# A Mamba-2 block and an ELU layer on one core: seven products in place of eight for half of the first two blocks' second layer, and 512-column products in their first layer

## The chip, the cores and the metric

The kernel runs on one core of one Trainium2 chip. A core has TensorE (PE: matrix products, with its weight loads listed as PEld), VectorE (DVE), ScalarE (ACT), GpSimd (POOL) and SyncE (SP), which here only issues DMA transfers. The engines run side by side, each working through its own instructions in order. The metric is the device time of one execution in microseconds (us); the time before is the median of three runs.

## The reference

```python
x = scan(x, a, B, C)          # (4, 8, 768, 32): Mamba-2 scan, state 16
x = x.transpose(0, 2, 1, 3).reshape(3072, 256)
h = x @ w_in                  # (3072, 256) @ (256, 2048)
g = np.where(h > 0.0, h, np.exp(np.minimum(h, 0.0)) - 1.0)
out = g @ w_out               # (3072, 2048) @ (2048, 256)
```

All is float32 (the inputs reach the chip as 64-bit words, and the kernel makes float32 of the weights). The change is in the last three lines.

## The kernel before

The 3072 tokens are cut into 12 blocks of 256 (NP = 12, BLK = 256). A block n goes through the scan, whose result is yT, then the first layer, the ELU and the second layer. The order of all work on every engine is written out by hand: the order in which the Python code issues instructions is the order in which each engine runs them. A tile of a pool with `bufs` buffers waits for the tile that had the buffer before.

**First layer.** The 2048 columns of w_in are 16 groups of 128. `l1(n, i)` (line 631) makes groups 2i and 2i+1 for block n into one PSUM tile ps_h of 128x512, two products (k = 0, 1) for each group, 256 tokens wide. With `parts=2` it does so in halves of 128 tokens. It appends (n, i, ps_h) to the list `lag`; `elu` (line 654) takes the oldest entry, does two ACT passes and one DVE pass (lines 652, 659, 661) and leaves `g_of[n, i]` (128x512) in SBUF. Each float32 product in the source is two PE instructions and two weight loads in the profile.

**Second layer, direct.** `l2(n, j)` (line 753) takes groups 2j and 2j+1 of block n: four products 256 columns wide into the single PSUM tile ps_o of pool p_o. After j = 7 ACT copies it to `ob` and SP stores it.

**Both layers by seven products (Strassen-Winograd).** Blocks 2 and 3, 4 and 5 and so on are taken as pairs: two blocks by two halves of the contraction by two halves of the columns, a 2x2 problem with seven products in place of eight. It needs sums of the stationary and of the moving operands: `sum_weights` (line 677) makes four additions (s3, a21, s2, s4) for each of the eight index pairs i of w_out (`a_out`, `s_out`) or of w_in (`a_in`, `s_in`); `sum_t1` and `sum_t2` (lines 786, 790) make the differences of the g quarters; `sum_y` (line 701) those of yT. `quarters` (line 778) names the four quarters of the g tiles of a pair. `second(n)` (line 798) is a generator for the pair n, n+1: for each half of the contraction it goes through the seven products r = 0 to 6, four index pairs i each, and yields after each i. At the end of an r it adds the result to `c_sum` in parts: additions that read PSUM on DVE, the others on POOL (line 812), two copies on ACT (lines 841, 853), and the differences of g that later products need on POOL (line 776). `front`, `mid` and `back` are the first layer by seven products, from n = 4 on.

**Order around the change.** First a loop of twelve steps issues the rest of the first layer of blocks 0 and 1, with the scan of block 2 and the conversion of weight pieces 5 to 10. A weight piece (`w_take`, `w_give`) is one of 16 (8 of w_in, 8 of w_out): two ACT passes, three DVE passes and one POOL addition. Then comes a loop over n = 2, 3 and i = 0 to 7: each step issues `l2(n - 2, i)` and `l1(n, i)` on PE, drains `lag` and does some scan work of later blocks: in n = 2 the pieces 11 to 15, decays on ACT and POOL (`decay`, lines 493, 498), head masks and transposes on DVE (`turn_part`); at the third step of n = 3 `scores`, `sums`, eight weighings and the states of blocks 4 and 5; at the seventh their `across` and `inside`, and after these `sum_y(4)`. `more_sums(i - 1)` in n = 3 makes the weight sums of both layers (w_out on DVE, w_in on POOL) and sum_t1(2, i - 1). After the loop POOL does sum_t2(2, 0), and from n = 4 on each stage interleaves the first layer of the pair n, n+1 with `second(n - 2)`; `store` (line 880) writes c_sum.

PSUM has seven buffers in pool p_a (ps_h, scores, sums, across, and every second product of `second`) and one in p_o (the direct ps_o, and the other products of `second`).

Of the kernel before, what the change touches and what calls it, by code (L numbers as in the profile page):

```python
# [28 lines left out]
def kernel(  # L29
# [598 lines left out]

    g_of = {}

    def l1(n, i, parts=1):

        ps = psum([P, 2, BLK], "ps_h")
        for j in range(2):
            m = 2 * i + j
            for part in range(parts):
                toks = slice(part * BLK // parts, (part + 1) * BLK // parts)
                for k in range(KC):
                    nc.tensor.matmul(  # L639
                        out=ps[:, j, toks], lhsT=w_in[:, k, m * P:(m + 1) * P],  # L640
                        rhs=yT[n // 2][:, k, n % 2].rearrange("p u i -> p (u i)")[:, toks],
                        start=(k == 0), stop=(k == KC - 1))
        lag.append((n, i, ps))

    lag = []
# [31 lines left out]
    def sum_weights(eng, a, s, i):  # L677
        for step in weight_steps(eng, a, s, i):
            step()
# [67 lines left out]
    def row_of(n):  # L747
        b, g = place(n)
        return b * S + g * BLK

    o_of = {}

    def l2(n, j, half=None):


        if j == 0 and half != 1:
            o_of[n] = p_o.tile([P, 2, DM], F32, tag="o", name="ps_o")
        for m in (2 * j, 2 * j + 1) if half is None else (2 * j + half,):
            for ts in range(2):
                nc.tensor.matmul(  # L760
                    out=o_of[n][:, ts], lhsT=g_of[n, j][:, m % 2, ts * P:(ts + 1) * P],
                    rhs=w_out[:, m], start=(m == 0 and ts == 0), stop=(m == MC - 1),
                    skip_group_check=True)
        if j == MC // 2 - 1 and half != 0:
            ob = ffn.tile([P, 2, DM], F32, tag="ob", name="ob", bufs=1)
            nc.scalar.copy(out=ob, in_=o_of.pop(n))
            r0 = row_of(n)
            nc.sync.dma_start(
                out=out[r0:r0 + BLK, :].rearrange("(t p) e -> p t e", p=P), in_=ob)

    t2_of = {}

    def sub(out, in0, in1):
        nc.gpsimd.tensor_tensor(out=out, in0=in0, in1=in1, op=ALU.subtract)  # L776

    def quarters(n, i):


        A, B = g_of[n, i], g_of[n + 1, i]
        if n < 4:
            return A[:, 0], A[:, 1], B[:, 0], B[:, 1]
        return A[:, 0], B[:, 0], B[:, 1], A[:, 1]

    def sum_t1(n, i, eng=nc.gpsimd):
        b11, b21, b12, b22 = quarters(n, i)
        eng.tensor_tensor(out=b12, in0=b12, in1=b11, op=ALU.subtract)  # L788

    def sum_t2(n, half):  # L790
        for i in range(4 * half, 4 * half + 4):
            t2_of[n, i] = ffn.tile([P, BLK], F32, tag="t2", name="t2", bufs=4)
            b11, b21, b12, b22 = quarters(n, i)
            sub(t2_of[n, i], b22, b12)

    c_of = {}

    def second(n, last=False):


        c = c_of[n] = ffn.tile([P, 2, 2, 2, P], F32, tag="c", name="c_sum", bufs=1)
        c11, c12, c21, c22 = (c[:, at, :, e] for e in range(2) for at in range(2))
        a11, a12, s1, a22 = a_out
        s2, s3, s4 = s_out
        for half in range(2):
            tmp = ffn.tile([P, 3, 2, P], F32, tag="tmp", name="p_sum", bufs=1)
            p1, p5, u = (tmp[:, r] for r in range(3))
            chunk = range(4 * half, 4 * half + 4)
# [5 lines left out]
            for r, a in enumerate((a11, a12, s1, s2, s3, a22, s4)):  # L814
# [25 lines left out]
                if r == 0:  # L840
                    nc.scalar.copy(out=p1, in_=ps)
                    for i in chunk:
                        b11 = quarters(n, i)[0]
                        sub(b11, t2_of[n, i], b11)
                    if half:
                        add(c11, c11, p1)
                elif r == 1:
                    add(c11, ps, c11 if half else p1)
                    for i in chunk:
                        b21 = quarters(n, i)[1]  # L850
                        sub(b21, b21, t2_of[n, i])
                elif r == 2:
                    nc.scalar.copy(out=p5, in_=ps)
                elif r == 3:
                    add(u, ps, p1)
                    add(p5, p5, u)
                    if half:
                        add(c22, c22, p5)
                        add(c12, c12, p5)
                elif r == 4:  # L860
                    add(c22, ps, c22 if half else p5)
                    add(u, ps, u)
                    if half:
                        add(c21, c21, u)
                    if last and half:
                        r0 = row_of(n + 1)
                        nc.sync.dma_start(
                            out=out[r0:r0 + BLK, P:2 * P].rearrange("(t p) c -> p t c", p=P),
                            in_=c22)
                    if not half:  # L870
                        sum_t2(n, 1)
                    elif n + 2 < NP:
                        sum_t2(n + 2, 0)
                elif r == 5:
                    add(c21, ps, c21 if half else u)
                else:
                    add(c12, ps, c12 if half else p5)
# [126 lines left out]
    write_flat(2)  # L1004

    todo = 5
    for s, (n, i) in enumerate((
            (1, 0), (1, 1), (1, 2), (0, 4), (1, 3), (0, 5), (1, 4), (0, 6), (1, 5), (0, 7),
            (1, 6), (1, 7))):
        l1(n, i, parts=2 if s < 2 else 1)  # L1010
        if s < 8:
            decay_of(2, s)
        if s == 7:
# [108 lines left out]
            at = k // 2 * 2 + late  # L1122
            turn_part(*[(m, 0), (m, 1), (m, 2), (m + 1, 0), (m + 1, 1), (m + 1, 2), (m, 3), (m + 1, 3)][at])

    def more_sums(i):
        sum_weights(nc.vector, a_out, s_out, i)
        sum_weights(nc.gpsimd, a_in, s_in, i)
        sum_t1(2, i, nc.vector)


    for n in (2, 3):
        for i in range(8):
            if n == 3 and i > 0:
                more_sums(i - 1)
            l2(n - 2, i)
            piece = todo < len(pieces) and (n, i) != (2, 1)
            if n == 2 and i == 0:
                elu()
            if piece:
                w_take(todo, nc.scalar if i > 1 else nc.vector)  # L1140
            end_of_two(n, 2 * i)
            l1(n, i)
            if n == 2 and i == 0:
# [9 lines left out]
            if n == 2:  # L1153
# [7 lines left out]
                        weigh(3, q)  # L1161
                if i == 2:
                    states(3)
                if i == 6:
                    inside(across(3), 3)
            else:
                if i == 0:
                    s_in[:], s_out[:] = weight_sums(), weight_sums()
            scan_ahead(n, i)
            end_of_two(n, 2 * i + 1)  # L1170
    sum_t2(2, 0)
    left = weight_steps(nc.vector, a_out, s_out, 7)

    for n in range(4, NP, 2):
        m = n + 2 if n + 2 < NP else None
# [13 lines left out]
        for k in range(16):  # L1189
# [29 lines left out]
                begin_elu()  # L1219
            else:  # L1220
                mid(n, i)
                if i == 0 and n > 4:
                    store(n - 4, 0)
                    store(n - 4, 1)
                begin_elu()
# [3 lines left out]
                next_elu()  # L1229
                begin_elu()  # L1230
                turn_step(n, k, True)
                if n == 4 and i < 4:
                    next(left)()
                    if i == 0:
                        sum_weights(nc.gpsimd, a_in, s_in, 7)
                        sum_t1(2, 7)
                if not m or i < 4:
                    l2s(1)
            if m:
# [42 lines left out]
```

## Time and profile before

| | |
|---|---|
| median of three runs | 356.01 us (355.25 to 356.28) |
| profiled execution, whole | 355.13 us |
| its span | 353.2 us |
| granted TensorE clock | 1.00 |
| second-layer products, direct, 128x256 (L760) | 128 instructions, 30.7 us |
| second-layer products, seven, 128x128 (L834) | 1104 instructions, 142.5 us |
| first-layer products, direct, 128x256 (L639) | 240 instructions, 56.5 us |
| first-layer products, direct, 128x128 (L639) | 32 instructions, 4.0 us |
| differences of g on POOL (L776, L788) | 153 operations, 109.7 us |
| the same on DVE (L788) | 7 operations, 3.4 us |

The profile is of one execution by the hardware profiler; its span leaves out 1.9 us of what the whole time counts. A row's busy time is what its instructions cover; matmuls overlap, so a row's mean is longer than its pace. In time, the loop of twelve steps ends at 52 us on PE, the steps of n = 2 run from 52 to 82.7, those of n = 3 from 82.7 to 114.8, and n = 4 begins there.

### The profile page before, as it was taken

How to read it: one execution, taken by the hardware profiler on the slowest of the kernel's cores; microseconds unless marked ns; L12 is line 12 of the kernel's file. 1: busy time of each engine (PE TensorE's matmuls, PEld its weight loads, DVE VectorE, ACT ScalarE, POOL GpSimd, SP SyncE). 2: the span in 40 equal slices, each digit the busy share in tenths (PEclk: the TensorE clock that was granted, in tenths of full speed). 3: DMA queues.
4: the chain of work that ended last, by engine and by line, in shares of the span. 5: the costliest groups of instructions: out<-in, count | busy, mean ns of one | idle time of the engine just before them, and what ended most of it. 6: DMA issues, size and time to landing. Idle time of an engine off the chain costs nothing.

```text
span 353.2 us, 9965 instructions
## 1 busy us (share of the span) xinstructions
PE 347.2 (98%) x3960; PEld 313.1 (89%) x3960; DVE 239.5 (68%) x497; ACT 204.8 (58%) x497; POOL 230.2 (65%) x365
## 2 busy tenths in 40 slices
PE   8899999999999999999999999999999999999996
PEld 5579788888888999999999999999999999999996
DVE  4998879863999768684677684677684565656212
ACT  4878989787435577535677535586635444535100
POOL 5454554553676997887377788468687545465883
PEclk9999999999999999999999999999999999999999
DMA  8878789572440500136500145600000100000101
GB/s 147 209 207 178 264 184 256 90 143 52 72 141 2 121 0 3 18 80 146 122 0 2 14 90 128 134 3 0 2 2 2 62 3 0 2 0 30 32 2 59
DMA packets 74542, 26.49 MB, mean 75 GB/s; under 512 B 59840, under 2 KB 69376, under 8 KB 74496
## 3 DMA queue, kind: packets, MB, share of 16 engines
q1 hardware_dynamic: 72176, 25.60, 31.5%
q8 instruction: 31, 0.51, 0.6%
q10 hardware_dynamic: 2320, 0.26, 0.5%
q14 instruction: 15, 0.12, 0.1%
HBM read 22.51 MB, written 3.34 MB: 73 GB/s over the span
## 4 chain that ended last, share of the span: by engine, by line
PE 87%; DVE 0%; issue 0%
PE ps_o L834 35%; PE ps_h L711 28%; PE ps_h L639 10%; PE ps_o L760 8%; PE ps_y L607 2%; PE ps_g L513 2%; PE ps_y L588 1%; PE ps_st L543 1%; PE ps_o L820 1%; DVE c_sum L823 0%; PE ps_tc L401 0%; PE ps_tb L401 0%
## 5 line engine op out<-in xcount | busy, mean ns | idle before, releaser
L652 ACT ACTIVATE e<-ps_h 128x512 f32<-128x512 f32 x96 | 57.2, 596 | 91.1 <-DVE ps_h L736 49.1
L834 PEld LDWEIGHTS ps_o<-w_out,g 128*128 128x128 f32 x640 | 79.9, 192 | 2.9
L834 PE MATMUL ps_o<-w_out,g 128*128 128x128 f32 x640 | 81.0, 275 | 0.0
L661 DVE SCALAR_TENSOR_TENSOR g<-e,ps_h 128x512 f32<-128x512 f32 x96 | 65.1, 680 | 14.2 <-ACT e L659 13.8
L659 ACT ACTIVATE e<-e 128x512 f32<-128x512 f32 x96 | 61.1, 636 | 2.0
L639 PE MATMUL ps_h<-yT,w_in 128*128 128x256 f32 (+1 forms) x272 | 60.4, 370 | 1.4 <-ACT w_in L192 0.9
L788 POOL TENSOR_TENSOR g<-g 128x256 f32<-128x256 f32 x33 | 24.0, 728 | 54.8 <-DVE g L661 54.7
L639 PEld LDWEIGHTS ps_h<-yT,w_in 128*128 128x128 f32 x272 | 48.5, 190 | 8.6 <-POOL w_in L230 2.1
L493 ACT ACTIVATE L<-L,ncum 128x64 f32<-128x64 f32 x160 | 41.3, 340 | 0.9 <-DMA L<-flat 0.8
L834 PE MATMUL ps_o<-w_sum,g 128*128 128x128 f32 x304 | 39.9, 275 | 0.0
L834 PEld LDWEIGHTS ps_o<-w_sum,g 128*128 128x128 f32 x304 | 38.5, 192 | 1.1
L744 DVE TENSOR_TENSOR ps_h<-ps_h,u_sum 128x512 f32<-128x512 f32 x32 | 22.4, 699 | 23.9 <-PE ps_h L711 23.7
L711 PE MATMUL ps_h<-yT,w_in 128*128 128x256 f32 x128 | 38.5, 383 | 0.0
L711 PE MATMUL ps_h<-y_sum,w_in 128*128 128x256 f32 x128 | 38.1, 380 | 0.0
L711 PE MATMUL ps_h<-y_sum,w_sum 128*128 128x256 f32 x128 | 38.1, 379 | 0.0
L498 POOL TENSOR_SCALAR_AFFINE_SELECT L<-L 64x512 f32<-64x512 f32 x40 | 28.0, 701 | 11.5 <-ACT L L493 10.2
L728 DVE TENSOR_TENSOR u_sum<-ps_h,u_sum 128x512 f32<-128x512 f32 x32 | 22.1, 690 | 14.7 <-ACT u_sum L721 11.0
L736 DVE TENSOR_TENSOR ps_h<-ps_h,u_sum 128x256 f32<-128x256 f32 x32 | 13.8, 433 | 25.7 <-PE ps_h L711 25.4
L760 PE MATMUL ps_o<-w_out,g 128*128 128x256 f32 x128 | 30.7, 382 | 0.0
L776 POOL TENSOR_TENSOR t<-g 128x256 f32<-128x256 f32 x40 | 28.9, 755 | 0.2
L776 POOL TENSOR_TENSOR g<-g,t 128x256 f32<-128x256 f32 x40 | 28.8, 753 | 0.2
L776 POOL TENSOR_TENSOR g<-t,g 128x256 f32<-128x256 f32 x40 | 28.0, 732 | 1.1 <-PE ps_o L834 1.1
(116 smaller groups left out, 535.4 us busy)
## 6 DMA issues: line engine op xcount, KB each, us to landing
L<-flat SPq DMA_DIRECT2D x20, 256.0 KB
w<-in_moe_w_out_dram SPq DMA_DIRECT2D x8, 512.0 KB
w<-in_moe_w_in_dram SPq DMA_DIRECT2D x7, 512.0 KB
xr<-in_x_dram SPq DMA_DIRECT2D x24, 128.0 KB
out_dram<-c_sum SPq DMA_DIRECT2D x9, 256.0 KB
bc<-in_B_dram SPq DMA_DIRECT2D x24, 64.0 KB
bc<-in_C_dram SPq DMA_DIRECT2D x22, 64.0 KB
ec<-flat_exp SPq DMA_DIRECT2D x10, 128.0 KB
```

The costliest lines, as they stand in the source:

```text
L493: nc.scalar.activation(L[:, h, u], L[:, h, u], ACT.Exp, bias=ncum[:, u, row:row + 1])
L498: nc.gpsimd.affine_select(out=part, in_=part, pattern=[[0, 4], [0, 2], [1, Q]], compare_op=ALU.is_ge, fill=0.0, base=0, channel_multiplier=-1)
L639: nc.tensor.matmul(out=ps[:, j, toks], lhsT=w_in[:, k, m * P:(m + 1) * P], rhs=yT[n // 2][:, k, n % 2].rearrange("p u i -> p (u i)")[:, toks],
L652: nc.scalar.activation(begun[0], lag[0][2], ACT.Relu, scale=-1.0)
L659: nc.scalar.activation(e, e, ACT.Exp, scale=-1.0)
L661: nc.vector.scalar_tensor_tensor(out=g_of[n, i], in0=e, scalar=1.0, in1=ps, op0=ALU.subtract, op1=ALU.max)
L711: nc.tensor.matmul(out=out, lhsT=lhsT, rhs=rhs, start=first, stop=True, skip_group_check=True)
L744: nc.vector.tensor_tensor(out=c2, in0=c2, in1=u[:, 0:2], op=ALU.add)
L760: nc.tensor.matmul(out=o_of[n][:, ts], lhsT=g_of[n, j][:, m % 2, ts * P:(ts + 1) * P], rhs=w_out[:, m], start=(m == 0 and ts == 0), stop=( ...
L776: nc.gpsimd.tensor_tensor(out=out, in0=in0, in1=in1, op=ALU.subtract)
L788: eng.tensor_tensor(out=b12, in0=b12, in1=b11, op=ALU.subtract)
L834: nc.tensor.matmul(out=ps[:, ts], lhsT=b[:, ts * P:(ts + 1) * P], rhs=a[:, i], start=(i == chunk[0] and ts == 0), stop=(i == chunk[-1]), s ...
```

## The change

1. Loop of twelve: the first four steps are `l1(1, 0)` to `l1(1, 3)`, without halves. The other eight are `l1_two(i, j)` for i = 4 to 7: one group, 2i + j, for blocks 0 and 1 together, in two products of 512 columns. g_of[0, i] then holds group 2i of both blocks and g_of[1, i] group 2i + 1 (`quarters` has a case for n = 0).
2. `l2` is direct for groups 0 to 7 only (j = 0 to 3), both blocks in the steps of n = 2. Its sum is copied to `c_sum` and not stored.
3. `second(0)` does the other half by seven products in the steps of n = 3, four yields in a step up to i = 3, then three. It adds to c_sum, and the pair is stored in the first step of n = 4.
4. The sums that it needs move: sum_t1(0, 4..7), sum_t2(0, 1) and the weight groups 4 to 6 of w_out go to DVE in the steps 4 to 7 of n = 2, group 7 to the start of n = 3, groups 0 to 3 to its steps 2 to 5. For n = 0 the four differences after r = 0 run on DVE. The first of the four additions of each w_in group goes to POOL in steps 4 to 7 of n = 2 (`in_first`), the other three (`in_rest`) stay in n = 3. sum_t2(2, 0) comes at the end of r = 4 of `second(0)`.
5. Weight pieces 12 to 15 are converted at steps 3 to 6 of n = 2 and not at 2 to 5.

```diff
+    def l1_two(i, j):
+        ps = psum([P, 2, BLK], "ps_h")
+        for k in range(KC):
+            nc.tensor.matmul(
+                out=ps, lhsT=w_in[:, k, (2 * i + j) * P:(2 * i + j + 1) * P],
+                rhs=yT[0][:, k].rearrange("p n u i -> p n (u i)"),
+                start=(k == 0), stop=(k == KC - 1))
+        lag.append((j, i, ps))
...
-        if j == MC // 2 - 1 and half != 0:
-            ob = ffn.tile([P, 2, DM], F32, tag="ob", name="ob", bufs=1)
-            nc.scalar.copy(out=ob, in_=o_of.pop(n))
...
+        if j == MC // 4 - 1:
+            if n == 0:
+                c_of[0] = ffn.tile([P, 2, 2, 2, P], F32, tag="c", name="c_sum", bufs=1)
+            nc.scalar.copy(
+                out=c_of[0][:, n].rearrange("p t e c -> p t (e c)"), in_=o_of.pop(n))
...
-        for half in range(2):
+        for half in range(2) if n else (1,):
...
-                        sub(b11, t2_of[n, i], b11)
+                        sub(b11, t2_of[n, i], b11, nc.gpsimd if n else nc.vector)
...
-        l1(n, i, parts=2 if s < 2 else 1)
+    for s in range(12):
+        if s < 4:
+            l1(1, s)
+        else:
+            l1_two(s // 2 + 2, s % 2)
...
-    def more_sums(i):
-        sum_weights(nc.vector, a_out, s_out, i)
-        sum_weights(nc.gpsimd, a_in, s_in, i)
-        sum_t1(2, i, nc.vector)
+    def in_first(i):
+        nc.gpsimd.tensor_tensor(
+            out=s_in[1][:, i], in0=a_in[0][:, i], in1=a_in[2][:, i], op=ALU.subtract)
+    def in_rest(i):
+        for k, step in enumerate(weight_steps(nc.gpsimd, a_in, s_in, i)):
+            if k:
+                step()
+    steps = second(0)
     for n in (2, 3):
         for i in range(8):
-            if n == 3 and i > 0:
-                more_sums(i - 1)
-            l2(n - 2, i)
+            if n == 2:
+                l2(i // 4, i % 4)
...
+            else:
+                if i == 0:
+                    sum_weights(nc.vector, a_out, s_out, 7)
+                for _ in range(4 if i < 4 else 3):
+                    next(steps)
+            piece = n == 2 and i in (0, 3, 4, 5, 6)
...
+                if i > 3:
+                    in_first(2 * i - 8)
+                    in_first(2 * i - 7)
+                if i > 3:
+                    sum_t1(0, i, nc.vector)
+                if i > 4:
+                    sum_weights(nc.vector, a_out, s_out, i - 1)
...
+                if i == 7:
+                    sum_t2(0, 1, nc.vector)
             else:
...
+                if i > 0:
+                    in_rest(i - 1)
+                    sum_t1(2, i - 1, nc.vector)
+                if 1 < i < 6:
+                    sum_weights(nc.vector, a_out, s_out, i - 2)
...
-    sum_t2(2, 0)
-    left = weight_steps(nc.vector, a_out, s_out, 7)
...
-                if i == 0 and n > 4:
+                if i == 0:
                     store(n - 4, 0)
                     store(n - 4, 1)
...
-                if n == 4 and i < 4:
-                    next(left)()
-                    if i == 0:
-                        sum_weights(nc.gpsimd, a_in, s_in, 7)
-                        sum_t1(2, 7)
+                if n == 4 and i == 0:
+                    in_rest(7)
+                    sum_t1(2, 7)
```

## The prediction, as put on record before the run

> **What bounds the kernel now.** I read the page's busy shares and chain first, then the list of what TensorE (PE) waited for, then busy time by windows around the change, then the order-of-time views of PE, VectorE (DVE) and GpSimd (POOL).
>
> ```profile
> PE 347.2 (98%) x3960; PEld 313.1 (89%) x3960; DVE 239.5 (68%) x497; ACT 204.8 (58%) x497; POOL 230.2 (65%) x365
> ...
> PE 87%; DVE 0%; issue 0%
> ```
> ```profile
> PE ps_idle L245 <- DVE idle L240: 1.1, 1, 1.1
> PE ps_h L639 <- ACT w_in L192: 0.9, 1, 0.9
> PE ps_h L639 <- POOL w_in L230: 0.5, 1, 0.5
> PE ps_st L543 <- DMA xr<-in_x_dram: 0.4, 1, 0.4
> ```
>
> PE sets the time: all that it ever waits for is 2.9 us, every wait lies before 23 us, and from there to 350 us one product follows another. So less PE work shortens the kernel one for one, and any new PE wait lengthens it one for one. The next question is which engine could make PE wait where the change is. The windows (start:end, length, then busy time and count for PE, PEld, DVE, ACT, POOL) show it:
>
> ```profile
> 72.40:82.70 10.30, 10.30 (x139) 8.80 (x138) 5.36 (x10) 8.63 (x26) 4.05 (x4) 1.00 0.72 129
> 82.70:93.20 10.50, 10.50 (x50) 8.96 (x49) 6.54 (x14) 6.57 (x18) 5.74 (x10) 1.00 0.34 65
> 93.20:104.00 10.80, 10.80 (x155) 9.48 (x155) 9.94 (x27) 3.69 (x6) 7.40 (x17) 1.00 0.51 131
> 104.00:114.80 10.80, 10.80 (x232) 9.38 (x231) 10.46 (x23) 5.27 (x11) 7.52 (x14) 1.00 0.02 5
> ```
>
> DVE is at 92% and 97% in the last two windows; its free time lies in the first two.
>
> **PE work, the gain.** One instruction of a direct product (128x256) takes 1.73/8 = 216 ns, one of a seven-product (128x128) 1.78/16 = 111.5 ns; both are paces in the chain in order of time (start, length, what):
>
> ```profile
> 113.27 1.73 PE ps_h L639 x8
> 115.00 1.29 PE ps_h L711 x6
> 116.29 1.78 PE ps_o L834 x16
> ```
> A product in the source is two instructions.
> - Second layer: eight calls of l2 go, 8 x 8 x 0.216 = 13.82 us. second(0) issues 7 products x 4 groups x 2 halves x 2 = 112 instructions, 12.49 us. Gain 1.33 us.
> - First layer, halves: 32 instructions of 128 columns become 16 of 256: 3.57 to 3.46 us. Gain 0.11.
> - First layer, 512 columns: 64 of 216 ns (13.82 us) become 32 of a kind that no warm row shows. Twice the 256-column price, 432 ns, gains nothing; going on by the step from 128 to 256 columns (104.5 ns per 128) gives 425 ns, a gain of 0.22; if a whole per-instruction part of 7 ns were saved twice the gain would be 0.45. I take 427 ns, near that straight line: 0.16 us.
> Sum: 1.60 us (1.44 to 1.89).
>
> The Trainium skill ("TensorE: Matmul & The Clock Gate", Back-to-back issue gap) gives N/2.4 + 2.5 ns for one pass; the 256-column row of 216 ns is two such passes (an estimate, 2 x 109), and 512 columns would be two passes of 215.8 ns, 432 ns. By the page the 512-column part would gain nothing and the sum would be 1.44.
>
> **What is added elsewhere.** On DVE, within steps 4 to 7 of n=2 and the whole of n=3: sum_t1(0,4..7), sum_t2(0,1) and the four subtractions after r=0 of second(0) are 12 operations on two SBUF halves (line 788's kind); six additions out of PSUM (line 812's kind, 0.36 us apart); the weight group 7 comes in from n=4 (4 operations of line 687). Three groups (4, 5, 6) move forward from n=3 into n=2. On POOL: five c additions, four subtractions of b21 and the four of sum_t2(2,0), 13 x 0.72 = 9.4 us, are new in n=3, and eight first weight differences move ahead into n=2; before n=4 these subtractions ran after the first products of that stage.
>
> The price of a two-SBUF-input operation on DVE depends on POOL:
>
> ```profile
> 91.75 0.29 DVE L687 TENSOR_TENSOR w_sum<-w_out 128x128 f32<-128x128 f32 x1
> 92.07 0.29 DVE L687 TENSOR_TENSOR w_out<-w_out 128x128 f32<-128x128 f32 x1
> ...
> 103.62 0.50 DVE L687 TENSOR_TENSOR w_out<-w_out 128x128 f32<-128x128 f32 x1
> 104.15 0.50 DVE L687 TENSOR_TENSOR w_sum<-w_out 128x128 f32<-128x128 f32 x1
> ...
> 113.39 0.70 DVE L687 TENSOR_TENSOR w_out<-w_out 128x128 f32<-128x128 f32 x1
> 114.12 0.70 DVE L687 TENSOR_TENSOR w_sum<-w_out 128x128 f32<-128x128 f32 x1
> ```
> ```profile
> 104.05 0.46 POOL L687 TENSOR_TENSOR w_sum<-w_in 128x128 f32<-128x128 f32 x1
> ...
> 113.90 0.77 POOL L706 TENSOR_TENSOR y_sum<-yT 128x256 f32<-128x256 f32 x1
> ```
> At 91.75 POOL is idle: 0.32 us from start to start. At 103.6 POOL runs 128-column additions: 0.53. At 113.4 it runs the 256-column y_sum: 0.73. So DVE gets one such operation in for each of POOL's. ELUs (line 661) keep their 0.61 us beside either.
>
> The Trainium skill says the same and harder ("SBUF", Who interferes with whom): a DVE instruction with two SBUF inputs and a GpSimd instruction that reads SBUF share a port, and the loser blocks for the whole instruction. This speaks against the change. Held strictly, every added pair would cost DVE the full 0.73 us; the row at 103.6 shows 0.53 beside shorter POOL work, and the sum goes by the rows.
>
> Four points where PE then waits; PE works in order, so all of its later work stands behind each:
>
> (1) The last of r=2's four groups, which needs the second operation of weight group 7 (n=3, step 0). On DVE, from the ELU that starts at 75.91 to there: 21 two-input operations, 3 ELUs (1.83), one head mask (0.62), the last weight piece, now a step later (1.47), two transposes (1.0). At 0.32 that is 11.7 us, ready at 87.6; at 0.53, 16.0 us, ready at 91.9; at 0.60 (between the 0.53 and 0.73 rows), 93.4. POOL's list for that time (two weight sums of 1.25, six differences of 0.53, four masks of 0.69, c 0.72, two scalings 1.2, four subtractions 2.9, three sums 1.6) is about 15 us, so it is busy nearly throughout. PE comes there at 82.5 + 2 x (1.78 + 1.73) + 1.34 = 90.8. Wait 0 to 3.7 (the top is 0.60 plus 1.1 us of waits of DVE on late ELUs and weight pieces); I take 2.0, between the ends 1.1 and 2.6 of the contended prices.
>
> (2) scores(4,5) needs the head mask of block 5, which is behind two weight operations, four subtractions and an ELU: 3.2 us at 0.32, 4.4 at 0.53, against 2.2 us of PE work. Wait 0 (if (1) does not bind) to 2.3; I take 1.5. Before, the mask was done 4 us ahead.
>
> (3) across(4,5) needs four of the seven PSUM buffers, one of them r=4's, freed by DVE's addition of u. From the head mask to it: 16 two-input operations, 8 weighings (2.7), 8 states (1.7), 4 ELUs (2.4), 4 additions (1.4), cts and transpose (1.5): 14.9 us alone, 18.3 contended, against 14.6 us of PE. Wait 0.3 to 3.7; POOL stands idle in part of this (it waits for the states), so I take 2.0.
>
> (4) The first y_sum product of n=4. POOL's queue from that addition of u on: c21 0.72, sum_t2(2,0) 2.9, six sums 3.2, two y_sums 1.5, together 8.3 us; PE from across on: 2.3 + 1.34 + 1.73 + 0.44 = 5.8. If (3) binds, the wait is 2.5; if DVE is on time (u 2.5 us before across), 0. I take 2.5.
>
> Sum 8.0 us of waits, 1.60 of gain: +6.4.
>
> **Edits costed at nothing.** Blocks 0 and 1 still take 12 ELUs in the loop of twelve; weights are needed one step later than before. ACT copies the direct sums into c_sum instead of ob (0.56 us either way). Pieces 12 to 15 are converted a step later; piece 15 lands about 83.4, used at 83.8, covered by r=0 and costing as much as DVE is later than that. The two stores move from SP at 81.8 and 113.9 to step 0 of n=4, after c12; behind them on SP are spread_exp and load_x for the next pair, not used before 147, and the next write of c_sum comes 9 us later (123.8); the stores issued at 166.5 kept nobody waiting at the next write 11 us later. Without that cover DVE would wait as it once does on such a store, 1.7 us. Four weight steps that leave n=4 free DVE there, which has idle time: nothing.
>
> **Sum against the runs.** The profiled execution took 355.13 us with a span of 353.2, so 361.5; it is 0.9 under the median 356.01, so I put the forecast at 356.0 + 6.4 = 362.4.
>
> **Rivals.**
> - DVE keeps up. Its idle time of some 8 us between 77 and 88 (2.14 + 3.64 + 2.21 before three ELUs) takes the 20 operations that are placed there at 0.32 (6.4 us), and all four waits vanish: 356.0 - 1.6 = 354.4. For: the sum fits at the price beside an idle POOL. Against: POOL is filled in the same steps, and at 0.53 they need 10.6. It decides if the two-input price stays under about 0.40.
> - Half of the contention: (1) and (2) nearly vanish, (3) leaves 0.5 and (4) 2.5: 356.0 - 1.6 + 3.0 = 357.4. For: the seven weight groups of n=3 took 12.6 us in all from their first operation to line 788's after them, 0.45 for each of 28, since POOL paused at times. Against: the pauses are what the change fills.
> - Gain and one short wait cancel, about 356.0: (4) alone at 1.6.
> - Full price: (1) 3.7, (2) 2.0, (3) 2.4, (4) 2.5, less 1.6: +9.0, 365.0. It is the top of the forecast's own case.
>
> **How the numbers follow.** Forecast with its top 0.60 (own range 359 to 366.5), half contention 0.20, cancelled 0.07, DVE keeps up 0.13. A measurement tells 0.3% (1.1 us) from no change: faster 0.13, same 0.07, slower 0.80. The range runs from 355.2, which leaves out the faster case, to 366.5, 1.5 above the full price.
>
> **What would show it.** Right: PE waits named after DVE in n=3 (ps_o for w_out's sums, ps_g for the head mask, ps_y) and after POOL's y_sum at the start of n=4; DVE busy over 95% from 76 us to there; line 788 on DVE near 0.5 to 0.6 us. Step sizes: 112 more instructions at line 834's kind, 64 fewer at 760, 32 of 512 columns near 427 ns in pace. Wrong: no PE wait between 80 and 125 us, or a loss after 130 us, where I see none. If line 788 on DVE stays at 0.42 the forecast falls to the rivals.

## The result, and the profile after

The changed kernel took 367.18 us (364.76 to 368.48, six runs), 1.0307 times the kernel before [1.0277, 1.0337]: slower by 11 us. A second set of runs of the same kernel, beside the later experiments, gave 365.24 us against 354.84, 1.0300 [1.0270, 1.0329]. The profiled execution took 368.22 us with a span of 366.5; the second one's span is 364.9. The document calls these two profiles the first and the second.

The first profile's page, busy shares, granted clock by fortieths of the span, and the chain that ended last:

```profile
PE 350.3 (96%) x3960; PEld 309.3 (84%) x3960; DVE 252.3 (69%) x515; ACT 204.4 (56%) x499; POOL 236.8 (65%) x374
...
PEclk9999989999999899999999999999999999999999
...
PE 73%; DVE 9%; POOL 2%; issue 2%; ACT 1%; DVEq 0%; POOLq 0%; ACTq 0%
```

PE's share of the chain fell from 87% to 73%, DVE's rose from 0% to 9%. The two 8s in the clock row, in the slices that begin at 46 and 119 us, are new. What PE waited for, in the same profile (total, times, longest):

```profile
PE ps_o L843 <- DVE w_out L695: 2.6, 1, 2.6
PE ps_h L647 <- POOL w_in L230: 2.5, 3, 1.7
PE ps_h L719 <- POOL y_sum L714: 1.6, 1, 1.6
PE ps_y L588 <- DVE p_sum L821: 1.5, 1, 1.5
PE ps_g L513 <- DVE cts L416: 1.4, 1, 1.4
PE ps_g L513 <- DVE g L669: 1.3, 1, 1.3
```

Four of them stand at the four places of the prediction, in the order (1), (4), (3), (2); the last, (2), names the ELU of line 669 and not the head mask. The other two, for w_in and cts, lie in and before the loop of twelve, where the prediction added none. The windows over n = 2's last steps and r = 0 to 2 (start:end, length, then PE, PEld, DVE, ACT, POOL, clock, DMA share, GB/s):

```profile
76.70:87.05 10.35, 10.35 (x140) 8.83 (x139) 10.18 (x18) 9.86 (x28) 5.98 (x8) 1.00 0.50 88
87.05:97.60 10.55, 8.72 (x61) 8.00 (x59) 10.31 (x20) 6.80 (x19) 9.35 (x14) 1.00 0.17 25
```

DVE is busy for 98% of both, where in the kernel before it was busy for 52% and 62% of the windows 72.40:82.70 and 82.70:93.20; PE idles for 1.8 us of the second. Now PE in order of time (start, length, what, idle before it):

```profile
46.70 6.57 PE L635 MATMUL ps_h<-yT,w_in 128*128 128x512 f32 x12
...
98.34 0.71 PE L843 MATMUL ps_o<-w_out,g 128*128 128x128 f32 x4 [2.57 <-DVE w_out L695]
...
119.49 0.80 PE L588 MATMUL ps_y<-cts,Sx 32*64 32x64 f32 x52 [1.46 <-DVE p_sum L821]
...
122.03 2.60 PE L843 MATMUL ps_o<-w_sum,g 128*128 128x128 f32 x12
...
128.38 0.70 PE L719 MATMUL ps_h<-y_sum,w_sum 128*128 128x256 f32 x2 [1.58 <-POOL y_sum L714]
```

The waits (1), (3) and (4) end at 98, 119 and 128 us. Twelve seven-product instructions take 1.34 us at 111.5 ns; the row at 122.03 shows 2.60, most of it at half the clock, and the 512-column products at 46.70 are slow in the same way (12 in 6.5 us; 5.35 in the second profile). The table shows where the time went, by starts of PE's work:

| us | before | first | second |
|---|---|---|---|
| n = 2 begins | 51.97 | 56.27 | 53.15 |
| n = 2 | 30.77 | 30.78 | 30.77 |
| n = 3, to the first y_sum product of n = 4 | 32.53 | 41.33 | 41.27 |
| from there to the end of the span | 237.93 | 238.12 | 239.71 |

They lose 8.8 and 8.7 us in n = 3, where the change put its work. The rest differs between executions: 4.3 us before n = 2 and 0.2 after n = 3 in the first, 1.2 and 1.8 in the second.

### The profile page after: what moved, and what is told of

Same layout as the page of the kernel before. It is cut to its first block, busy times and chain, and to the rows that moved or that the text cites. A ratio compares the mean times of both kernels' runs of the same rounds, so it can differ in the third digit from the quotient of the medians.

```text
span 366.5 us, 9989 instructions
## 1 busy us (share of the span) xinstructions
PE 350.3 (96%) x3960; PEld 309.3 (84%) x3960; DVE 252.3 (69%) x515; ACT 204.4 (56%) x499; POOL 236.8 (65%) x374
## 4 chain that ended last, share of the span: by engine, by line
PE 73%; DVE 9%; POOL 2%; issue 2%; ACT 1%; DVEq 0%; POOLq 0%; ACTq 0%
PE ps_o L843 35%; PE ps_h L719 27%; PE ps_h L635 2%; PE ps_h L647 2%; DVE w_sum L695 2%; PE ps_g L513 1%; PE ps_o L768 1%; PE ps_y L607 1%; DVE g L797 1%; PE ps_st L543 1%; DVE g L669 1%; DVE w_out L695 1%; POOL t L783 1%; PE ps_y L588 1%; DVE g L783 1%
## 5 line engine op out<-in xcount | busy, mean ns | idle before, releaser
L843 PEld LDWEIGHTS ps_o<-w_out,g 128*128 128x128 f32 x704 | 87.9, 192 | 5.9 <-DVE w_out L695 2.8
L843 PE MATMUL ps_o<-w_out,g 128*128 128x128 f32 x704 | 89.4, 276 | 2.6 <-DVE w_out L695 2.6
L797 POOL TENSOR_TENSOR g<-g 128x256 f32<-128x256 f32 x33 | 24.0, 727 | 57.1 <-DVE g L669 57.1
L647 PE MATMUL ps_h<-yT,w_in 128*128 128x256 f32 x192 | 45.6, 382 | 3.4 <-POOL w_in L230 2.5
L843 PE MATMUL ps_o<-w_sum,g 128*128 128x128 f32 x336 | 45.3, 279 | 0.0
L843 PEld LDWEIGHTS ps_o<-w_sum,g 128*128 128x128 f32 x336 | 43.6, 196 | 1.4 <-issue 0.2
L647 PEld LDWEIGHTS ps_h<-yT,w_in 128*128 128x128 f32 x192 | 35.3, 190 | 9.0 <-POOL w_in L230 4.5
L719 PE MATMUL ps_h<-yT,w_in 128*128 128x256 f32 x128 | 38.5, 383 | 0.0
L736 DVE TENSOR_TENSOR u_sum<-ps_h,u_sum 128x512 f32<-128x512 f32 x32 | 22.1, 690 | 16.4 <-ACT u_sum L729 11.3
L783 POOL TENSOR_TENSOR g<-g,t 128x256 f32<-128x256 f32 x44 | 32.0, 758 | 1.2 <-DVE t L783 1.0
L719 PEld LDWEIGHTS ps_h<-y_sum,w_sum 128*128 128x128 f32 x128 | 24.2, 190 | 5.2 <-POOL y_sum L714 2.0
```

The costliest lines, as they stand in the source:

```text
L647: nc.tensor.matmul(out=ps[:, j], lhsT=w_in[:, k, m * P:(m + 1) * P], rhs=yT[n // 2][:, k, n % 2].rearrange("p u i -> p (u i)"), start=(k = ...
L719: nc.tensor.matmul(out=out, lhsT=lhsT, rhs=rhs, start=first, stop=True, skip_group_check=True)
L736: nc.vector.tensor_tensor(out=u[:, 1:3], in0=c2, in1=u[:, 0].unsqueeze(1).to_broadcast([P, 2, BLK]), op=ALU.add)
L783: eng.tensor_tensor(out=out, in0=in0, in1=in1, op=ALU.subtract)
L843: nc.tensor.matmul(out=ps[:, ts], lhsT=b[:, ts * P:(ts + 1) * P], rhs=a[:, i], start=(i == chunk[0] and ts == 0), stop=(i == chunk[-1]), s ...
```

## The experiments

The theory: DVE falls behind, because its two-SBUF-input operations run at POOL's pace, and the four PE waits follow. Rivals: the first layer's part costs something by itself; the order of work on DVE or POOL makes the waits, not its amount; the lower clock after waits is the loss, not the waits. All ratios are to the kernel before on the same chip.

| kernel | median us | ratio [95%] | span |
|---|---|---|---|
| e1_first_only | 368.14 | 1.0376 [1.0330, 1.0422] | 366.3 |
| e2_second_only | 372.17 | 1.0480 [1.0436, 1.0523] | 371.4 |
| e3_no_dve_diffs | 360.41 | 1.0162 [1.0119, 1.0205] | 358.5 |
| e4_no_win_sums | 358.03 | 1.0088 [1.0057, 1.0118] | 355.9 |
| e1p_first_padded | 355.03 | 0.9995 [0.9978, 1.0011] | 352.7 |
| e2p_second_padded | 367.73 | 1.0355 [1.0320, 1.0391] | 366.2 |
| e5_pool_order | 360.58 | 1.0177 [1.0141, 1.0212] | 358.7 |
| e7_fill_wait | 364.21 | 1.0269 [1.0236, 1.0303] | 361.9 |
| c_after | 365.24 | 1.0300 [1.0270, 1.0329] | 364.9 |
| e8_dve_order | 366.97 | 1.0324 [1.0278, 1.0371] | 366.1 |
| e9_mask_on_act | 366.78 | 1.0337 [1.0298, 1.0375] | 362.6 |
| e10_before_no_halves | 355.24 | 1.0013 [0.9978, 1.0048] | 353.0 |
| c_e5 | 360.00 | 1.0148 [1.0122, 1.0174] | 358.4 |
| e11_fill_waits | 362.21 | 1.0210 [1.0176, 1.0245] | 360.6 |

**One half of the change at a time.** e1 is the kernel before with the new loop of twelve; e2 is the changed kernel with the old loop.

```diff
 # e1, on the kernel before (and l1_two; l2 reads g_of[m % 2, j][:, n] for n < 2, j > 3)
+    for s in range(12):
+        if s < 4:
+            l1(1, s)
+        else:
+            l1_two(s // 2 + 2, s % 2)
 # e2, on the changed kernel
+        l1(n, i, parts=2 if s < 2 else 1)
```

> The 512-column products of the first layer alone; the second layer of blocks 0 and 1 direct as before. Theory A (the loss comes from DVE and POOL being late in n=2, n=3 and the start of n=4, and from a half clock after one of the waits; the late start of n=2 in the changed kernel's profile is a late weight piece and a late DMA of ec in that one execution): 355.5 to 356.5 us, no PE wait after 45 us. Theory B (the first-layer part itself delays the loop of twelve, with a wait of some 1.4 us for cts and a half clock after it): 358.5 to 360 us, with that wait and the half clock in the profile.

> The second-layer part alone; the loop of twelve as before. Theory A: 363 to 366.5 us, the four waits (w_out sum, ctm, p_sum, y_sum) of 6 to 8 us in all, as in the changed kernel. Theory B: 362 us or less, since the 3 us of the loop of twelve are gone.

Both lost more than the whole change, which no sum of the two parts allows. What PE waited for in e1 was new, and so is its place, the middle of the dense products of `inside` (e1's PE in order of time):

```profile
110.61 1.05 PE L607 MATMUL ps_y<-M,xr 64*32 64x64 f32 x82
113.59 0.83 PE L607 MATMUL ps_y<-M,xr 64*32 64x64 f32 x46 [1.93 <-issue]
114.35 3.41 PE L770 MATMUL ps_o<-w_out,g 128*128 128x256 f32 x8
```
PE stood still after 82 of 128 products (in the kernel before, all 128 run in 1.51 us), waiting for no engine and no transfer that the profile shows, and went on at half the clock (8 products in 3.41 us, against 1.89). This happens four times in e1, 8.1 us in all, and in e2 three times at that line, 5.2 us, and once at another, 2.1. The page of the kernel before lists a queue of instruction loads (pieces, MB):

```profile
q8 instruction: 31, 0.51, 0.6%
```
That is 16.4 KB a piece. The kernel before and the changed one have the same x3960 on PE (3960 products and 3960 weight loads); 7920 instructions over 31 pieces are 255 a piece, so I take the queue for PE's and a piece for 256 instructions. e1 has x3912, so 96 instructions less, and e2 x4008, 96 more. That would move every later boundary between pieces by 96 instructions. A guess from this: a piece that has to arrive while 256 short instructions run comes too late.

**The same halves, with the boundaries put back.** Products of the first layer in halves of 128 columns fill up the count: e1p has x3960 again, e2p x4088 (256 instructions more than the kernel before, one piece; its page lists 32).

```diff
 # e1p, on e1
-            l1(1, s)
+            l1(1, s, parts=2)
...
-            l1(n, i)
+            l1(n, i, parts=2 if n == 2 and i < 2 else 1)
 # e2p, on e2
-        l1(n, i, parts=2 if s < 2 else 1)
+        l1(n, i, parts=2)
```

> As e1_first_only (13 us slower, with PE standing still for 1.9 to 3.2 us in the middle of line 607 and no releaser), but six calls of l1 go in halves of 128 tokens, so that PE's instruction count is that of the kernel before (3960 products and 3960 weight loads). Theory F (the standstills are PE waiting for its own code, which comes in pieces of 256 instructions, 31 of 16 KB; they appear where a piece ends inside a dense run of small products, so the 96 instructions that e1 had less moved the ends there): no standstill, 354.5 to 356.5 us. Theory B (the wide products cause them): standstills stay, 362 us or more.

> As e2_second_only (17 us slower), but all twelve l1 of the loop of twelve go in halves, some 1.2 us more PE work, so that PE has 256 instructions more than before when it comes to n=3 and its pieces of code end where they ended before. Theory F: no standstill; the four waits on DVE and POOL stay at 5 to 8 us: 361 to 366 us. Rival (the second-layer part brings the standstills by itself): they stay, 371 us or more.

The standstills in `inside` are gone from both (e2p has one of 0.8 us at another line, 453). e1p, 13 us faster than e1 with more PE work, can't be told from the kernel before: the first layer's part is worth 0, within -0.2% and +0.1%. e2p came out above what was expected of it: it has the waits for w_out (2.6), the ELU ahead of the head mask (1.3) and y_sum (2.8) with half the clock after the last two, and its padding costs about 1.3 us (sixteen 128-column products in 1.83 us, eight of 256 in 1.73, twelve times). So the loss is the second layer's, and the guess on the boundaries held. In e1p's order of time, eight 512-column products start at 34.03 and what follows them at 37.47: 430 ns each, twice the 215 of 256 columns.

**Which engine is late.** e3 leaves out the twelve differences of g on DVE for blocks 0 and 1 (its second layer for them is computed from other operands); e4 leaves out all sums of w_in on POOL, so the first layers from n = 4 on are computed with other weights.

```diff
 # e3
-                    sum_t1(0, i, nc.vector)
...
-                    sum_t2(0, 1, nc.vector)
+                    for q in range(4, 8):
+                        t2_of[0, q] = quarters(0, q)[3]
...
-                        sub(b11, t2_of[n, i], b11, nc.gpsimd if n else nc.vector)
+                        if n:
+                            sub(b11, t2_of[n, i], b11)
 # e4 (in_first and in_rest do nothing)
-                    s_in[:] = weight_sums()
+                    s_in[:] = [a_in[1], a_in[2], a_in[1]]
```

> The changed kernel without the twelve differences of g that it adds on DVE (sum_t1(0), sum_t2(0,1) and the four after r=0 are left out, so the products read other data). Theory A1 (DVE is late because it has too many operations): these took some 10.8 us of DVE in the changed profile, more than the lateness, so the waits for the w_out sum and for ctm vanish and the y_sum wait stays in part: 358 to 361 us. Theory A2 (the lateness comes mostly from POOL holding DVE up at each operation): 362 to 365 us.

> The changed kernel without the 32 sums of w_in on POOL (left out; the first layer's products read parts of w_in in their place); DVE has every operation that it has in the changed kernel. Theory A1 (number of DVE operations): the waits for the w_out sum and ctm stay over 2.5 us in all; only the y_sum wait goes: 363 to 366 us. Theory A2 (POOL holds DVE up): line 695's operations on DVE fall from about 0.5 to 0.35 us, those waits fall under 1.5 us, and the y_sum wait goes: 358 to 361 us.

What PE waited for beyond its start, e3 first:

```profile
PE ps_h L719 <- POOL y_sum L714: 2.8, 1, 2.8
PE ps_y L588 <- DVE p_sum L821: 1.5, 1, 1.5
```
```profile
PE ps_o L843 <- DVE w_out L695: 1.9, 1, 1.9
...
PE ps_y L588 <- DVE p_sum L821: 0.6, 1, 0.6
PE ps_g L513 <- DVE g L669: 0.5, 1, 0.5
```

Twelve operations less on DVE take away waits (1) and (2) and leave (3) and (4). POOL's weight sums less take away (4) and shorten the other three by 0.7 to 0.9 us each, though none of DVE's own work was removed. Both halves of the theory show, DVE's amount of work and POOL's pace. Neither takes the loss away alone.

DVE's price can be read where it waits on POOL, in the first profile (start, length, what; DVE, then POOL):

```profile
87.49 1.22 DVE L797 TENSOR_TENSOR g<-g 128x256 f32<-128x256 f32 x1
...
97.59 0.69 DVE L695 TENSOR_TENSOR w_out<-w_out 128x128 f32<-128x128 f32 x1
...
105.62 0.29 DVE L695 TENSOR_TENSOR w_out<-w_out 128x128 f32<-128x128 f32 x1
```
```profile
87.15 1.27 POOL L230 TENSOR_TENSOR w_out<-mag,w_out 128x512 uint32<-128x512 uint32 x1 [2.31 <-DVE mag L220]
```

A difference of g on DVE takes 1.22 us beside the 1.27-us addition with which POOL ends a weight piece. Three of the four of sum_t1(0, 4..7) meet such an addition (1.22, 1.20, 1.22 and 0.52). All twelve differences take 9.25 us, 0.77 each. The 21 operations of step (1) lie between 81.46 us and 98.28, where the w_out one ends; without the six other operations there that is 12.7 us from start to start, 0.60 each. Beside an idle POOL the weight operation takes 0.29.

**The order on POOL.** e5 puts y_sum(4) ahead of sum_t2(2, 0) and of the last four groups of w_in's sums, which go to n = 4's first steps.

```diff
-                    in_rest(i - 1)
+                    if i < 5:
+                        in_rest(i - 1)
...
+            if (n, i) == (3, 6):
+                sum_t2(2, 0)
...
-                    in_rest(7)
+                if n == 4 and i < 4:
+                    in_rest(4 + i)
```

> The changed kernel with POOL's order alone altered: y_sum(4) ahead of sum_t2(2,0) and of the w_in sums 4 and 5. Theory A (the y_sum wait is POOL's queue behind a late DVE addition): the wait at the start of n=4 falls from 1.6 to under 0.5 us, the waits for the w_out sum, ctm and p_sum stay: 0.8 to 2 us faster than the changed kernel, 365 to 366.5 us. Rival (the order doesn't matter, since PE then waits for what was moved back): no change, 367 us or more.

> The kernel of e5_pool_order once more, to stand beside the next one on the same chip: 359.5 to 362 us, waits of 2.6 us (w_out sum) and 1.3 us (ctm), and one stretch at half clock after them.

This is the one rearrangement that paid: 1.0177 and, again, 1.0148, against 1.0307 and 1.0300, some 5 us. Wait (4) is gone in both profiles. Wait (3) was gone from the first, where (1) and (2) stayed at 2.6 and 1.3 us, and back at 1.5 us in the second, so only (4) can be put down to the order. From n = 3's start to the first y_sum product it is 38.26 and 38.15 us, 3.1 less than in the changed kernel, and no half clock follows at the start of n = 4.

**The order on DVE.** e8 is e5 with the third and fourth additions of groups 4 to 7 of w_out, the differences of g and groups 0 to 3 each moved back, towards the place where they are needed (group 3 into n = 4); e9 is e8 with the head masks of blocks 5 and 6 on ACT. c_after is the changed kernel again, beside them.

```diff
 # e8, on e5
-                    sum_weights(nc.vector, a_out, s_out, i - 1)
+                    out_steps(i - 1, (0, 1))
...
-                if i == 7:
-                    sum_t2(0, 1, nc.vector)
+                if i == 7:
+                    out_steps(7, (0, 1))
...
+                if i == 1:
+                    sum_t2(0, 1, nc.vector)
+                if i == 5:
+                    for q in range(4, 8):
+                        out_steps(q, (3,))
 # e9, on e8
+        if n in (5, 6):
+            for k in range(2):
+                nc.scalar.mul(s["ctm"][:, :, k], s["ct"], hmask2[:, k:k + 1])
+            return
```

> The changed kernel with POOL's order of e5 and another order on DVE, with every operation kept: of the weight groups 4 to 7 only what r=2 needs comes ahead of r=2, the rest, sum_t2(0,1) and the differences after r=0 come later, groups 0 to 2 at steps 3, 6 and 7 of n=3 and group 3 in n=4. Theory A (order decides which PE work is late, the amount of DVE work decides how much): the waits for the w_out sum and ctm fall under 0.5 us each, no half clock after them, a wait later (p_sum, or front_sums in n=4) of 1 to 4 us: 355 to 359 us. Rival (the amount decides all): 360 us or more, the waits only moved.

> As e8, with the head masks of blocks 5 and 6 made on ACT (two operations each), 1.5 us less for DVE. Theory A: 0.5 to 1.5 us under e8. Rival: as e8, if what is left isn't DVE's lateness.

> The changed kernel unaltered, on the same chip as the next three. Theory S (of the 11 us, some 3 us came from a slower start in that job: a late weight piece, then the late ec and a half clock after it): 362.5 to 365.5 us here. Otherwise 366 to 368 us.

Nothing was won. PE's waits in e8:

```profile
PE ps_o L843 <- DVE g L783: 3.8, 1, 3.8
PE ps_h L719 <- DVE u_sum L736: 2.8, 1, 2.8
PE ps_o L843 <- DVE w_sum L695: 1.7, 1, 1.7
```

Waits (1) and (2) are gone, and 3.8 us at 103 us, 1.7 at 115 and 2.8 at 129 have come, all on DVE: the differences after r = 0 are too late for r = 4, the fourth additions for r = 6, and in n = 4 DVE is late with u_sum. e9 has the same three. Both are 6 us slower than e5, whose order on POOL they share, though DVE has no more to do before n = 4. So the waits only moved, as the rival had it, but its reason, that the amount decides all, isn't shown: this order was the worse one, and two head masks less on DVE made no difference that could be measured.

**Work in place of the waits.** To see what the lower clock costs, e7 puts three extra products of 256 columns ahead of r = 6 of `second(0)`, and e11 (on e5) eight ahead of r = 2. Their results are overwritten by the first product of the group.

```diff
 # e11; e7 the same with r == 6 and 3 products
+                if n == 0 and r == 2:
+                    for _ in range(8):
+                        nc.tensor.matmul(
+                            out=ps.rearrange("p t c -> p (t c)"), lhsT=w_out[:, 8, 0:P],
+                            rhs=quarters(n, chunk[0])[3], start=True, stop=True,
+                            skip_group_check=True)
```

> The changed kernel with three more 256-column products (1.3 us of PE work, results overwritten) just before the products of r=6 of second(0), shortly ahead of the place where PE waits 1.5 us for p_sum and then runs 3.4 us at half clock. Theory C (the half clock follows from PE's standing still there, and costs some 1.7 us): the wait is nearly filled, the clock stays at 1.00 there, and the kernel is 0.5 to 2 us faster than the changed one, in spite of more work. Rival (the half clock has nothing to do with the wait): as slow or up to 1.3 us slower, with the half clock still there.

> The kernel of e5 with eight more 256-column products (3.5 us of PE work, overwritten) ahead of r=2 of second(0), where PE otherwise stands still for 2.6 and then 1.3 us. Theory C (standing still brings the half clock, which costs 1.7 us): no half clock there, the two waits fall to 0.6 us or less in all, and the kernel is 1 to 2 us faster than c_e5 although it does more. Rival (the half clock comes from something else, or costs nothing since DVE is late anyway): within 0.6 us of c_e5 or slower.

e7 filled wait (3), and no half clock came there; it came at 100 us instead, after wait (2). Its 1.0269 isn't clear of the changed kernel's 1.0307 and 1.0300. In e11 the granted clock is 1.000 over the whole span, against 0.995 in c_e5 on the same chip. Yet it isn't faster. PE in order of time, c_e5 and then e11:

```profile
93.49 1.22 PE L843 MATMUL ps_o<-w_out,g 128*128 128x128 f32 x4 [2.59 <-DVE w_out L695]
94.50 2.82 PE L647 MATMUL ps_h<-yT,w_in 128*128 128x256 f32 x8
...
120.00 0.59 PE L719 MATMUL ps_h<-yT,w_in 128*128 128x256 f32 x2
```
```profile
90.61 3.62 PE L841 MATMUL ps_o<-g,w_out 128*128 128x256 f32 x16
...
121.19 0.59 PE L719 MATMUL ps_h<-yT,w_in 128*128 128x256 f32 x2
```

From the start of r = 2 (89.40 in c_e5, 90.61 in e11) to the first product of n = 4 it is 30.60 and 30.58 us. c_e5 runs at half the clock after its wait, and in e11 PE is in time but then waits for DVE at the next places (0.7 for the ELU, 1.4 for p_sum). While DVE is the late one, the lower clock between two of its waits is free. e11's other 2 us lie elsewhere: it began r = 2 1.2 us later, with 1.0 us for a transfer of xr, and took 1.0 us more after the start of n = 4, 0.7 of it a standstill without a releaser.

**The halves alone.** e10 is the kernel before without the halves of the loop's first two steps, 32 instructions fewer on PE.

```diff
-        l1(n, i, parts=2 if s < 2 else 1)
+        l1(n, i)
```

> The kernel before with its two l1 in halves made whole: 16 products fewer on PE, less than 0.3 us of work. Theory F: the ends of the pieces of code move 16 products deeper into line 607; with some 4.3 us since the end before there is no standstill or one under 1 us at each of four places: 354.5 to 358 us. Rival (only moves of 48 or more matter, or something other than code loading): 354.5 to 355.5 us.

Its ratio holds 1, and its profile has one standstill of 0.5 us. A shift of the boundaries by 32 instructions did no harm that could be measured. One by 96 cost 13.1 us in e1 (against e1p) and 4.4 in e2 (against e2p, with its padding).

## Why the prediction was right in direction and short in size

**The gain on PE.** The second layer's 1.33 us follows from the counts and the paces, and both paces held in the rows outside waits (16 seven-products in 1.79 us, eight direct ones in 1.73). The 512 columns were taken at 427 ns; measured 430 and more, so no gain. The halves' 0.11 us can't be seen in e1p or e10. The gain was 1.33, not 1.60.

**The four waits.** All four came, at the places named. The time lost at each, from the start due to the start seen in the first profile, stands beside the forecast. The last column adds the time by which PE's rows since the wait before were slower than the same rows of the kernel before (scores, states and the first groups of r = 0 and r = 3, 0.9 us; `across`, `inside` and twelve products at the lower clock, 1.5). It estimates the wait of a PE that keeps its pace, which is what the prediction priced:

| wait | forecast | lost | at PE's pace |
|---|---|---|---|
| (1) w_out's sums, due 95.61, seen 98.34 | 2.0 | 2.73 | 2.9 |
| (2) "head mask", due 100.82, seen 102.45 | 1.5 | 1.63 | 1.6 |
| (3) p_sum, due 117.83, seen 119.49 | 2.0 | 1.66 | 2.4 |
| (4) y_sum, due 126.64, seen 128.38 | 2.5 | 1.74 | 3.3 |
| sum | 8.0 | 7.76 | 10.2 |

10.2 less 1.33 is 8.9, the 8.8 of n = 3. The rows' own idle times add to 6.91, since a record goes on a little after the next start would have been due. In the second profile (2) is absent, (4) is 2.8, and the rows add to 6.87.

**Wait (2) ended on another operation.** The first profile, all engines in order of time:

```profile
101.72 0.68 DVE L669 SCALAR_TENSOR_TENSOR g<-e,ps_h 128x512 f32<-128x512 f32 x1
...
102.32 0.87 DVE L433 TENSOR_TENSOR ctm<-bct,hmask 128x512 f32<-128x512 f32 x1
...
102.45 1.49 PE L513 MATMUL ps_g<-ctm,bct 32*64 32x128 f32 x58 [1.30 <-DVE g L669]
...
103.24 0.46 PEld L513 LDWEIGHTS ps_g<-ctm,bct 32*64 32x64 f32 x32 [0.36 <-DVE ctm L433]
```

Scores went on when the ELU had read its PSUM tile, 0.7 us before the mask was done; the mask held up a weight load by 0.36 us. Scores takes four of the seven PSUM buffers, and PE stopped after three products (six instructions), ahead of the first that writes the fourth tile; so a buffer was missing, as the prediction had it for (3). The ELU stands just ahead of the mask on DVE, behind the same late work, so that the size of (2) came near the forecast was partly luck.

**DVE's price.** Line 788 on DVE (L797 after) was forecast near 0.5 to 0.6 us. It was 1.2 in three cases of four. The rows of before beside which it was priced had POOL at 128 and 256 columns; the 512-column additions at L230, also in the moved steps, were not set beside it. Over the 21 operations of step (1) the price was 0.60, the upper of the prediction's two contended prices, with which its own working gives 2.6; it took 2.0, midway to the 1.1 of 0.53. DVE also began these steps 0.65 us later than the shift of the whole explains.

**What failed: "Sum 8.0 us of waits", and two places put at nothing.** The mechanism was right, and the sum was short: the four waits are worth 10.2, near the 10.6 of the "full price", above all by (1), at the upper price, and by (4), where POOL's queue from u on took 9.0 us and not 8.3 and PE had 5.6 us of work and not 5.8. The gain was 0.27 us less than put. With both, n = 3 costs 8.8 us in place of the 6.4 of "Sum 8.0 us of waits, 1.60 of gain: +6.4". That alone would have stayed inside the range. The rest lies where the prediction had no term: before n = 2 (4.3 and 1.2 us in the two profiles) and after the last wait (0.2 and 1.8).

What PE does between the waits doesn't enter. In both profiles DVE has no idle time from 74 us until the last c_sum addition of n = 3 is done, so it sets when (1), (2) and (3) end, and POOL behind it when (4) ends. In the first profile PE ran at half the clock after wait (3) (PEclk is the third number from the end), in the second after (1) and (4):

```profile
120.00:122.00 2.00, 2.00 (x147) 1.79 (x143) 1.93 (x4) 0.80 (x3) 2.00 (x4) 0.69 0.03 8
122.00:124.00 2.00, 2.00 (x13) 1.97 (x10) 1.97 (x4) 1.41 (x4) 1.92 (x4) 0.50 0.00 0
```
The second, PE in order of time:
```profile
95.10 1.22 PE L843 MATMUL ps_o<-w_out,g 128*128 128x128 f32 x4 [2.58 <-DVE w_out L695]
96.11 3.00 PE L647 MATMUL ps_h<-yT,w_in 128*128 128x256 f32 x8
...
116.25 0.80 PE L588 MATMUL ps_y<-cts,Sx 32*64 32x64 f32 x52 [1.46 <-DVE p_sum L821]
...
125.19 0.79 PE L719 MATMUL ps_h<-y_sum,w_sum 128*128 128x256 f32 x2 [2.83 <-POOL y_sum L714]
125.77 1.06 PE L719 MATMUL ps_h<-y_sum,w_in 128*128 128x256 f32 x2
126.62 3.12 PE L843 MATMUL ps_o<-w_out,g 128*128 128x128 f32 x16
```

Yet n = 3 takes 41.33 and 41.27 us, and 41.34 in e2, with a standstill of 1.5 us ahead of (4), 41.42 in e2p and 41.37 in e7, with three more products: the waits that follow make up the difference. After (4) DVE waits for PE again (2.39 us at 126.94 in the second profile), and the half clock there is lost time, 1.8 us from 125 to 130 us. The prediction looked for no loss after 130 us; this one lies just ahead of that, and its sum has no term for it.

**The loop of twelve.** The prediction has no cost there, and "every wait lies before 23 us" was read from the list of waits. The list hides one: before, the scores at 41.33 took 1.62 us for 32 instructions, which take 0.69 in e1p, because the transfer of ec came 0.61 us late to DVE's cts. There was no margin. PE and DVE before, then DVE in the first profile:

```profile
41.33 1.62 PE L513 MATMUL ps_g<-ctm,bct 32*64 32x128 f32 x32
```
```profile
41.20 0.42 DVE L416 TENSOR_TENSOR cts<-ps_tc,ec 128x256 f32<-128x256 f32 x1 [0.61 <-DMA ec<-flat_exp]
```
```profile
44.10 0.42 DVE L416 TENSOR_TENSOR cts<-ps_tc,ec 128x256 f32<-128x256 f32 x1 [2.19 <-DMA ec<-flat_exp]
```

In the first profile PE waited 1.36 us for cts. By PE's starts, 1.6 us were lost before the scores, where a piece of w_in came late, 1.4 at the scores, and 1.3 by half the clock from 46 us: 4.3 in all. In the second profile the same place lost 1.2. e1p and e3 had no such wait, e2, with the old loop, one of 0.7, so the part depends on when transfers land in an execution. How often it comes was not settled.

**The rivals.** "DVE keeps up" needed two-input operations under 0.40 us, and the 0.60 over step (1) rules it out. "Half of the contention" (357.4) and "full price" (365.0) stood on the right and the wrong side: n = 3 alone, 8.8 us on 356.0, is the full price to 0.2 us. The measured 367.2 lies 2.2 above it and just above the range, by the late transfers ahead of n = 2 and the clock after (4), which no case held.

**Open.** What exactly sets off the half clock: in the first profile a wait of 2.57 us at 96 us did not and one of 1.46 at 118 did; in the second, 2.58 at 92.5 did. No version with the second layer's seven products beat the kernel before: of e5, e8 and e9 the best, e5, is 1.5 to 1.8% slower.

## What to carry to other kernels

Price lateness on the engine that is late: here DVE and POOL made n = 3 41.3 to 41.4 us long in five profiles, whatever PE's clock, standstills and extra products were. What follows the last such wait, 1.8 us of lower clock in one profile, comes on top. Before moving work to an engine with spare time, look at what its neighbour does in those same steps, at the largest operation and not the mean, and give the work whose result is needed first the first place in that neighbour's queue (5 of 11 us came back that way). When one part of a change is tried alone and costs more than the whole, look for a standstill without a releaser, and repeat it with the engine's instruction count put back.

## What the runs showed of the hardware

**Instruction loading.** A count of PE instructions that differs by 96 put standstills of up to 3.2 us into dense runs of 64-column products, 8.1 us in e1 and 7.3 in e2 (2.1 of these at a 256-column product), with the lower clock after two of the four in e1 and one of the four in e2; the same code, padded to a whole number of pieces from the old count, had none there. Pieces are of 16.4 KB (0.51 MB in 31). The Trainium skill ("Advanced Engine Details and Errata", ISA Cache) gives cache lines of 16 KB for 256 instructions, which is the size seen here. That a late piece is the cause is inferred from the place and from the padding; the profile names no releaser.

**Lower clock.** In the first profile a stretch at 0.50 lasts about 3.4 us: in the two windows shown and the next, at 0.96, 0.62 + 1.00 + 0.08 = 1.70 us of clock is missing, twice that is 3.4. In e8 the stretch at the wait of 3.8 us is twice as long, 3.4 us of clock missing from 100 to 110 us. Stretches followed PE waits of 1.3 to 3.8 us, not all of them. The Trainium skill ("TensorE: Matmul & The Clock Gate", Part 1: The HAM clock gate) has half rate after an idle window of about 3.4 us; only e8's 3.8 and e9's 3.7 were that long, and the length of the stretch agrees with its window. Kernels without waits in mid-span (before, e1p, e10) showed a granted clock of 1.000 in their profiles, and so did e4 (waits up to 1.9) and e11.

**DVE beside POOL.** In the first profile the price of a DVE operation with two SBUF inputs followed the length of the POOL operation beside it: a weight operation 0.29 us beside none and 0.4 to 0.8 beside 128 and 256 columns, a difference of g 0.41 beside none and 1.2 beside 512. Without the sums of w_in on POOL (e4) the waits for DVE fell by 0.7 to 0.9 us each.
